# Query stacks of an attention kernel: three heads in four copied straight from the halves, one by DRAM; key steps, the weight step and one subtraction placed anew

## The chip, the core and the metric

One core of a Trainium2 chip runs the whole kernel. TensorE is PE in the profile (PEld is its weight load), VectorE is DVE, ScalarE is ACT, GpSimd is POOL; SyncE, SP, issues nearly all DMAs here, in the order of its program. The metric is the device time of one execution in microseconds (us), the median of several runs.

## The reference, cut to what matters

```
for s in range(4):                       # segments of L = 512 tokens, H = 32 heads of 32
    logits = einsum("bhqd,bhkd->bhqk", qs, ks) * scale + mask      # mask: causal
    a_dot  = softmax(logits) @ vs
    pq     = phi(qs);  a_mem = (pq @ M) / (pq . z + 1e-6)
    o_s    = g * a_mem + (1 - g) * a_dot                            # g = sigmoid(beta), per head
    pk     = phi(ks);  M += pk^T vs;  z += sum(pk)
h  = x + concat(o) @ wo                  # q, k, v = layernorm(x) @ wq, wk, wv
h2 = h + MLP(layernorm(h))               # layernorm, 1024 -> 3584, gelu, 3584 -> 1024
```

All is float32: x has 2048 tokens of 1024 numbers.

## The kernel before, in words

A number is carried as a high part, rounded to the type that PE multiplies fast, and a low part, the rest; a product of two such numbers takes three multiplications (high by high, high by low, low by high). The tokens go in two halves of 1024. Each half has an attention stage and an MLP stage; the change touches only the attention.

An attention stage is a row of 16 units: 8 groups g of four heads, and for each the two segments of the half (sl 0 and 1). `dense` makes the projections of one unit in 24 steps of three 512-column multiplications: steps 0 to 7 keys (kps), 8 to 15 queries (qps), 16 to 23 values (vps). Beside them, step by step, `heads` works the four heads of the unit before: a slot of six steps for each head (`slot`), with the head in three successive slots. The four products of a head's queries and keys (pqk, q0 to q3 in the table, of 128, 384, 256 and 512 columns) stand in its first slot; then come the transposes of the softmax (ptr), and in a third slot the products with the values (av, tile po). PLAN lists what the six steps of a slot hold. For pqk, PE has two banks; DVE frees them (it adds the mask and takes the minimum, mx), ACT then takes the exponential (pr).

The query product needs three multiplications as well. They are done in one by stacking: a query stack has 96 rows, three for each of the 32 numbers of a head, (high, high, low), and the key stack (high, low, high). `stack` builds them. It writes the three sources for all four heads into a DRAM tensor of rows (r, b), three writes of 256 KB, and reads one stack of 96 rows for each head, four reads of 192 KB. The halves (qh, ql, kh, kl) come out of ACT and DVE from qps or kps: `queries` runs at step 16, `keys` at step 8.

The table TIMES says at which of a unit's steps the other work stands (a number of 24 or more lies in the next unit): ks and qs the stacks, kx the turn of phi(k) (DVE transposes in blocks of 32, writes to turn_dram, reads back four times), vx the same for the values (sch<-vps, turn_dram<-sch, sch<-turn_dram), vs the cast of the values' high part on ACT, vl the subtraction for the low part, lk, lq, lv and ck, cq, cv the loads and casts of the next group's weights (wr, wh, and wl on POOL). `weigh`, once in a unit, transposes the softmax denominators rs on PE (pw), writes them to r_dram and reads them back spread over partitions.

The order written in the program isn't the final one. A scheduler places each engine's instructions, DMA issues too, by when it expects their inputs; each engine then runs its own list in order, and waits where an input is late.

Of the kernel before, what the change touches and what calls it, by code (L numbers as in the profile page):

```python
# [17 lines left out]
P = 128  # L18
S = 2048
# [10 lines left out]
RA, RH, RS, PD, PS = 1.3, 14, 0.7, 20, 3  # L30
VT, KT, OT = True, True, True
WLC = 8
TIMES = dict(pk=10, kx=15, pkh=21, pkl=22, ks=16, qs=16, pq=16, pqh=20, pql=20, omt=20, vx=24, pm=25, vs=32, vl=33, pmm=40, om=35, omc=40, od=62, lk=13, lq=16, lv=20, ck=18, cq=22, cv=28)
PLAN = ('r', 'q0', 'a0 S2 t0 q2 s0', 'a1 q1', 't1 w q3', 't2 o s1')
SCALE = DH ** -0.5
EPS = 1e-5
DEN_EPS = 1e-6
# [5 lines left out]
def raw(ap):  # L43
    return ap.bitcast(F32)


def build(tc, x, wq, wk, wv, wo, beta, w1, b1, w2, b2, out):
    nc = tc.nc
# [5 lines left out]
    def ps_dense(name):  # L54
        return psum.tile([P, 512], F32, tag="d", name=name, bufs=3)

    PKL, VSL, GTE, WHK, WHQ, WHV = nc.gpsimd, nc.gpsimd, nc.gpsimd, nc.scalar, nc.vector, nc.scalar
    ident = const.tile([P, P], F32, name="ident")
    make_identity(nc, ident)
    hsel = const.tile([P, 76], F32, name="hsel")[:, 0:4]  # L60
# [23 lines left out]
    o_dram = [dram.tile([NG, P, 512], F32, name=f"o_dram{s}") for s in range(4)]  # L84
# [109 lines left out]
    def hooked(gen, fn, every, count):  # L194
        for n, _ in enumerate(gen):
            if n % every == every - 1 and n // every < count:
                fn(n // every)
            yield
# [152 lines left out]
    def attention(half, first):  # L351
# [4 lines left out]
        def tmp(name):  # L356
            return ab.tile([P, 512], F32, tag="tmp", name=name, bufs=5)
# [3 lines left out]
        def turned(src, to, mid):  # L361

            nc.vector.transpose(mid.rearrange("p (c k d) -> p c k d", c=4, k=4), src.rearrange("p (k c d) -> p c k d", c=4, k=4))
            d = turn_dram[acts.get("turned", 0) % len(turn_dram)]
            acts["turned"] = acts.get("turned", 0) + 1
            nc.sync.dma_start(d, mid)
            for c in range(4):
                nc.sync.dma_start(to[32 * c:32 * c + 32].rearrange("j (h x) -> j h x", h=4),
                                  d[:, c * P:(c + 1) * P].rearrange("(h j) x -> j h x", h=4))

        def tmpr(name):
# [19 lines left out]
        def stack(a, b, name, order):  # L391
            out = []
            n = acts[name] = acts.get(name, 0) + 1
            d = s_dram[name][n % 2]
            for blk, src in enumerate(order):
                nc.sync.dma_start(d[:, blk], raw((a, b)[src]))
            for j in range(4):
                st = ab.tile([96, 512], F32R, tag=name, name=name, bufs=5)
                nc.sync.dma_start(raw(st), d[32 * j:32 * j + 32].rearrange("r b n -> (r b) n"))
                out.append(st)  # L400
            return out

        small = []
# [20 lines left out]
        def dense(g, sl, ws, u):  # L424
# [24 lines left out]
            def key_stack():  # L449
                u["ks"] = stack(v["kh"], v["kl"], "ks", (0, 1, 0))  # L450
# [5 lines left out]
            def key_turn():  # L456
                v["kn"] = scr[1][:, 2 + sl]
                turned(v["pk"], v["kn"], scr[1][:, 0])
# [29 lines left out]
            def query_stack():  # L488
                u["qs"] = stack(v["qh"], v["ql"], "qs", (0, 0, 1))
# [97 lines left out]
            if g < NG - 1:  # L587
                on("od", partial(out_store, u))
                if sl == 1:
                    nxt = u["next"]  # L590
                    for n, w in (("k", wk), ("q", wq), ("v", wv)):
                        on("l" + n, partial(load_weight, nxt, n, w, g + 1))
                        on("c" + n, partial(cast_weight, nxt, n))
# [79 lines left out]
        def weigh(st):  # L673
            u, j = st["u"], st["j"]
            if j < 3:
                return
            n = acts["weighed"] = 1 - acts.get("weighed", 0)
            w = u["w"] = tmp("w") if u["g"] == NG - 1 and u["s"] % 2 else scr[n][:, 1]
            pw = ps_dense("pw")
            nc.tensor.transpose(pw[0:16, 0:P], u["rs"][:, 0:16], ident)  # L680
            nc.scalar.copy(w[0:16, 0:P], pw[0:16, 0:P])
            d = r_dram[n]
            nc.sync.dma_start(d, w[0:16, 0:P])
            for k in range(4):
                nc.sync.dma_start(w[32 * k:32 * k + 32, :],
                                  bass.AP(tensor=d.tensor, offset=d.offset + 512 * k, ap=[[0, DH], [1, 512]]))

        def ptr(st, n):
# [58 lines left out]

        def out_store(u):
            assert u["done"]
            nc.sync.dma_start(o_dram[u["s"]][u["g"]], u["w"])  # L750

        pipe = [None, None]

        def slot(cur):
            p1, p2 = pipe

            def call(st, fn, *args):
                if st:
                    fn(st, *args)

            ops = {"q": (cur, qk), "r": (p1, inverse), "w": (p1, weigh), "t": (p1, ptr), "s": (p1, sub), "S": (p2, sub),
                   "a": (p2, av), "o": (p2, av_out)}
            for step in PLAN:
                for op in step.split():
                    call(ops[op[0]][0], ops[op[0]][1], *[int(c) for c in op[1:]])
                yield
            pipe[0], pipe[1] = cur, p1

        def heads(u):
            for j in range(4):  # L770
                yield from slot({"u": u, "j": j})

        def tail():
            yield from slot(None)
            yield from slot(None)

        def weights(g):
            ws = {}
# [4 lines left out]

        def load_weight(nxt, n, w, g):
            wr = nxt[n] = wp.tile([P, DC, P], F32, tag="wr", name="wr", bufs=2)
            nc.sync.dma_start(wr, w[:, g * P:(g + 1) * P].rearrange("(c p) n -> p c n", p=P))

        def cast_weight(nxt, n):
            wr = nxt[n]
# [8 lines left out]
        for g in range(NG):  # L798
            for sl in range(2):
                u = {"g": g, "s": 2 * half + sl, "T": TIMES, "v": {}, "next": {}}  # L800
                d = dense(g, sl, ws, u)
# [6 lines left out]
                else:  # L808
                    if g == NG - 1 and sl == 1:
                        d = hooked(d, lambda k: load_o(half, 0, k, ab), 3, NG - 1)  # L810
# [647 lines left out]
    for half in range(2):  # L1458
        acts["zt"] = zt = tc.alloc_tile_pool(name=f"zt{half}", bufs=1, side="right")
        attention_pool(half)  # L1460
        first = None if half else opening()
        rest = attention(half, first)
        hts = [lnp.tile([P, D], F32, tag="ln", name="ht0", bufs=4) for _ in range(4)]
        ab = acts["ab"]
# [47 lines left out]
        order = ExitStack()  # L1512
# [84 lines left out]
```

## Time and profile before

| | us |
|---|---|
| median of 3 runs (lowest, highest) | 2323.99 (2323.52, 2328.03) |
| profiled execution | 2326.8 |
| its span, first to last instruction | 2324.9 |
| attention of the first half (about 16 units) | 60 to 549 |
| attention of the second half | 920 to 1400 |
| granted TensorE clock over the span | 0.995 |

In rows of groups, "x128 | 31.2, 244 | 33.7 <-..." reads: 128 instructions, 31.2 us busy, 244 ns each in the mean, 33.7 us in which the engine stood idle just before them, and what ended that idle time. In rows of time the first number is the start in us from the span's start, the second the length; a bracket gives idle time just before. A DMA row on SP (SPq) is the issue alone, "x4" four of them; the transfer itself runs on.

### The profile page before, as it was taken

The numbers are of one execution on the slowest core, as the hardware profiler recorded it, in microseconds if no ns is written. First come the engines' busy times: TensorE is split into PE (matmuls) and PEld (weight loads), VectorE is DVE, ScalarE is ACT, GpSimd is POOL, SyncE is SP. The second block draws the span as 40 slices with busy tenths as digits, with TensorE's granted clock in tenths as the row PEclk, the third lists the DMA queues.
The fourth block names the chain that finished last, engine by engine and source line by source line (L and its number), as shares of the span: only waits on it lengthen the run. The fifth ranks groups of instructions, "written<-read, shape, count | busy, mean of one in ns | idle before, by whom it ended". The sixth has DMA issues, their size and how long they took to land.

```text
span 2324.9 us, 34571 instructions
## 1 busy us (share of the span) xinstructions
PE 2257.8 (97%) x11481; PEld 1863.1 (80%) x11481; DVE 1516.8 (65%) x3041; ACT 1232.6 (53%) x2553; POOL 887.5 (38%) x742
## 2 busy tenths in 40 slices
PE   7999999999999999999999999999999999999999
PEld 6878877777788888788788877788887888888887
DVE  6767777776564565677777776574566666467663
ACT  5767777775363444677777775363344223322221
POOL 4323333333253443333333333244445654155430
PEclk9999999999999999999999999999999999999999
DMA  8656565664475656666666664466567976476772
GB/s 246 193 179 195 182 181 180 186 212 151 151 220 170 198 147 187 207 188 189 186 189 198 199 206 140 163 200 194 154 193 253 350 241 222 145 257 223 246 235 93
DMA packets 406940, 456.26 MB, mean 196 GB/s; under 512 B 30030, under 2 KB 264042, under 8 KB 406762
## 3 DMA queue, kind: packets, MB, share of 16 engines
q1 hardware_dynamic: 343594, 417.34, 57.1%
q10 hardware_dynamic: 63168, 36.71, 5.2%
q8 instruction: 91, 1.49, 0.3%
q14 instruction: 87, 0.71, 0.1%
HBM read 306.28 MB, written 147.65 MB: 195 GB/s over the span
## 4 chain that ended last, share of the span: by engine, by line
PE 73%; DMA 11%; DVE 4%; ACT 4%; POOL 3%; issue 2%; SPq 2%; ACTq 0%; POOLq 0%; DVEq 0%
PE po L1431 19%; PE bps L1035 9%; PE cps L1035 7%; PE dps L1035 6%; PE po L721 4%; PE ppt L701 4%; DMA qs_dram<-ql 3%; PE pqk L651 3%; PE qps L122 2%; PE qps L123 2%; PE qps L124 2%; DMA qs<-qs_dram 2%; PE kps L122 2%; PE kps L123 2%; PE pwo L123 2%
## 5 line engine op out<-in xcount | busy, mean ns | idle before, releaser
L660 ACT ACTIVATE pr<-pr,mx 128x128 f32<-128x128 f32 (+3 forms) x512 | 289.0, 564 | 147.5 <-DVE mx L652 143.2
L652 DVE CUSTOM_DVE_ANT_0 pr<-pqk,mask 128x128 f32<-128x128 f32 (+3 forms) x512 | 246.4, 482 | 107.0 <-PE pqk L651 102.6
L708 DVE TENSOR_TENSOR ptl<-ppt,pth 128x512 fp32r<-128x512 f32 (+1 forms) x384 | 225.7, 596 | 39.0 <-ACT pth L703 35.6
L703 ACT CAST pth<-ppt 128x512 fp32r<-128x512 f32 (+1 forms) x384 | 195.1, 512 | 69.1 <-PE ppt L701 66.0
L701 PE MATMUL ppt<-ident,pr 128*128 128x128 f32 x1280 | 220.7, 278 | 0.0
L651 PE MATMUL pqk<-ks,qs 96*128 96x128 f32 (+3 forms) x512 | 183.5, 360 | 34.5 <-DMA qs<-qs_dram 25.3
L1441 DVE TENSOR_TENSOR c<-c,po 128x512 f32<-128x512 f32 x160 | 105.3, 683 | 149.9 <-PE po L1431 147.3
L701 PEld LDWEIGHTS ppt<-ident,pr 128*128 128x128 f32 x1280 | 165.0, 141 | 35.8 <-issue 1.4
L794 POOL TENSOR_TENSOR wl<-wr,wh 128x1024 fp32r<-128x1024 f32 x42 | 100.3, 2388 | 189.9 <-ACT wh L792 156.4
L721 PE MATMUL po<-ptl,vs 128*64 128x512 f32 (+3 forms) x512 | 154.0, 310 | 0.4 <-DVE ptl L708 0.3
L721 PE MATMUL po<-pth,vs 128*64 128x512 f32 (+3 forms) x512 | 148.1, 310 | 0.7 <-POOL vs L531 0.7
L651 PEld LDWEIGHTS pqk<-ks,qs 96*128 96x128 f32 x512 | 98.5, 193 | 51.7 <-DVE ptl L708 22.8
L1431 PE MATMUL po<-w2h,zh 128*128 128x512 f32 x378 | 120.9, 389 | 0.2 <-DVE zh L1371 0.2
L1288 POOL TENSOR_TENSOR w2r<-w2r 128x512 f32<-128x512 f32 x54 | 87.1, 1625 | 73.8 <-DMA w2r<-in_B_w 73.8
L1035 PE MATMUL bps<-zh,sb 128*128 128x512 f32 x336 | 111.0, 391 | 0.0
L1035 PE MATMUL bps<-zh,sa 128*128 128x512 f32 x336 | 110.8, 390 | 0.0
L122 PE MATMUL kps<-yh,wh 128*128 128x512 f32 (+1 forms) x264 | 109.3, 414 | 0.0
L122 PE MATMUL qps<-yh,wh 128*128 128x512 f32 x256 | 108.0, 422 | 0.1
L122 PE MATMUL vps<-yh,wh 128*128 128x512 f32 x256 | 106.1, 415 | 0.0
L1431 PE MATMUL po<-w2h,hl 128*128 128x512 f32 x322 | 103.1, 390 | 0.2 <-DVE hl L1371 0.2
L123 PE MATMUL kps<-yl,wh 128*128 128x512 f32 (+1 forms) x264 | 102.9, 390 | 0.1
L124 PE MATMUL kps<-yh,wl 128*128 128x512 f32 (+1 forms) x264 | 102.8, 389 | 0.0
(251 smaller groups left out, 6533.6 us busy)
## 6 DMA issues: line engine op xcount, KB each, us to landing
hr<-h_dram SPq DMA_DIRECT2D x112, 448.0 KB, 5.5
w2r<-in_B_w SPq DMA_DIRECT2D x122, 256.0 KB, 4.4
r<-in_B_w SPq DMA_DIRECT2D x56, 512.0 KB, 4.5
ks<-ks_dram SPq DMA_DIRECT2D x128, 192.0 KB, 3.4
qs<-qs_dram SPq DMA_DIRECT2D x128, 192.0 KB, 4.1
h_dram<-ht ACTq DMA_DIRECT2D x84, 256.0 KB, 3.5
ks_dram<-kh SPq DMA_DIRECT2D x64, 256.0 KB, 2.4
qs_dram<-qh SPq DMA_DIRECT2D x64, 256.0 KB, 3.3
```

What stands on the lines that cost most here:

```text
L122: nc.tensor.matmul(ps, ah, bh, start=first, stop=False)
L123: nc.tensor.matmul(ps, ah, bl, start=False, stop=False)
L124: acts["mm"] = nc.tensor.matmul(ps, al, bh, start=False, stop=last)
L651: nc.tensor.matmul(pqk[:, :n], u["qs"][j][:, i * P:(i + 1) * P], u["ks"][j][:, 0:n], start=True, stop=True)
L652: nc.vector.tensor_tensor_reduce(out=st["pr"][:, offs[i]:offs[i] + n], in0=pqk[:, :n], in1=mask[:, 512 - n:512], op0=ALU.add, op1=ALU.min, ...
L660: nc.scalar.activation(pi, pi, AF.Exp, bias=mx[:, i:i + 1], scale=-1.0, accum_out=mx[:, 4 + i:5 + i])
L701: nc.tensor.transpose(ppt[:, o:o + P], pr[:, offs[i] + jk * P:offs[i] + (jk + 1) * P], ident)
L703: acts["pth"] = n, nc.scalar.copy(pth[:, base:base + w], ppt[:, :w])
L708: nc.vector.tensor_tensor(o, x0, x1, op=ALU.subtract)
L721: nc.tensor.matmul(po[:, P * jk:], v, st[part][:, koff[jk]:koff[jk] + w], start=(jk, part) == (0, "pth"), stop=(jk, part) == (2, "ptl"))
L1035: nc.tensor.matmul(ps, x_[:, c, :], y_[:, c, :], start=first and c == 0 and n == 0, stop=last and c == 3 and n == 2, skip_group_check=True)
L1431: nc.tensor.matmul(ps, x_[:, k], y_[k], start=opens and k == 0 and i == 0, stop=closes and k == self.KP - 1 and i == 2, skip_group_check=True)
```

## The change

The query stacks of the first three heads of a unit (QD = 3) are no longer read from DRAM. For each, three DMAs of 32 rows (64 KB) copy a head's rows of qh, qh and ql out of their tiles into every third partition of the stack. For the fourth head, its 32 rows alone are written to the DRAM tensor (three writes of 64 KB) and read back as one stack. That is 13 DMAs a unit in place of 7. Key stacks go by DRAM as before (KD = 0).

The key stack stands at step 11 instead of 16, the key turn at 12 instead of 15. PLAN is replaced by the table HEAD, whose numbers are 6 times the slot, plus the step, plus the place in the step; it holds the same order but for `weigh`, which moves from step 4 to step 3. The values' low part (VSL) is subtracted on DVE instead of POOL. The queue names BQ, TQ, LQ and OQ are all SP, as before.

```
-TIMES = dict(pk=10, kx=15, pkh=21, pkl=22, ks=16, qs=16, ...
-PLAN = ('r', 'q0', 'a0 S2 t0 q2 s0', 'a1 q1', 't1 w q3', 't2 o s1')
+TIMES = dict(pk=10, kx=12, pkh=21, pkl=22, ks=11, qs=16, ...
+HEAD = dict(r=6.1, q0=1.1, a0=14.1, s2=14.2, t0=8.3, q2=2.4, s0=8.5, a1=15.1, q1=3.2, t1=10.1, w=9.2, q3=4.3, t2=11.1, o=17.2, s1=11.3)
+KD, QD = 0, 3
...
-    PKL, VSL, GTE, WHK, WHQ, WHV = nc.gpsimd, nc.gpsimd, nc.gpsimd, nc.scalar, nc.vector, nc.scalar
+    PKL, VSL, GTE, WHK, WHQ, WHV = nc.gpsimd, nc.vector, nc.gpsimd, nc.scalar, nc.vector, nc.scalar
...
-            for blk, src in enumerate(order):
-                nc.sync.dma_start(d[:, blk], raw((a, b)[src]))
+            direct = {"ks": KD, "qs": QD}[name]
             for j in range(4):
                 st = ab.tile([96, 512], F32R, tag=name, name=name, bufs=5)
-                nc.sync.dma_start(raw(st), d[32 * j:32 * j + 32].rearrange("r b n -> (r b) n"))
                 out.append(st)
+                if j < direct:
+                    for blk, src in enumerate(order):
+                        nc.sync.dma_start(raw(st).rearrange("(r b) n -> b r n", b=3)[blk], raw((a, b)[src][32 * j:32 * j + 32, :]))
+            if direct < 4:
+                for blk, src in enumerate(order):
+                    nc.sync.dma_start(d[32 * direct:, blk], raw((a, b)[src])[32 * direct:])
+            for j in range(direct, 4):
+                nc.sync.dma_start(raw(out[j]), d[32 * j:32 * j + 32].rearrange("r b n -> (r b) n"))
...
+            states = [cur] + pipe
+            for step in range(6):
+                for _, op in sorted((t % 6, op) for op, t in HEAD.items() if int(t) % 6 == step):
+                    st = states[int(HEAD[op]) // 6]
+                    if st:
+                        fns[op[0]](st, *[int(c) for c in op[1:]])
```

How the scheduler places it: SP's list, in the second half of a unit of the first attention, from the reads of the key stacks to those of the turned values (sch). Before:

```order
L399 DMA ks<-ks_dram_164 96x512 x3
L368 DMA scl<-turn_dram_157 32x4x128 x4
L399 DMA ks<-ks_dram_164 96x512
L396 DMA qs_dram_166<-qh 128x512 x2
L396 DMA qs_dram_166<-ql 128x512
L399 DMA qs<-qs_dram_166 96x512 x4
L366 DMA turn_dram_158<-sch 128x512
L368 DMA sch<-turn_dram_158 32x4x128 x4
```

And with the change, in the same unit, from the pieces on (the rows ahead are the key reads and scl<-turn_dram):

```order
L403 DMA qs<-qh 32x512 x2
L403 DMA qs<-ql 32x512
L403 DMA qs<-qh 32x512 x2
L403 DMA qs<-ql 32x512
L403 DMA qs<-qh 32x512 x2
L403 DMA qs<-ql 32x512
L406 DMA qs_dram_166<-qh 32x512 x2
L406 DMA qs_dram_166<-ql 32x512
L368 DMA turn_dram_159<-sch 128x512
L691 DMA r_dram_161<-sch 16x128
L408 DMA qs<-qs_dram_166 96x512
L370 DMA sch<-turn_dram_159 32x4x128 x4
```

The three pieces of a head stand together, head by head; the four reads that stood ahead of turn_dram<-sch are one, behind it.

DVE's list, where the low part of the values now stands; pk is phi(k) of the next unit, pr,mx<-pqk the work that frees a bank of pqk. Before, then with the change:

```order
L708 TENSOR_TENSOR ptl<-ppt,pth 128x512
L388 SCALAR_TENSOR_TENSOR pk,zc<-e,r 128x512
L652 ISA pr,mx<-pqk,mask 128x256
L652 ISA mx 128x1
L363 STREAM_TRANSPOSE scl<-pk 128x512
```

```order
L716 TENSOR_TENSOR ptl<-ppt,pth 128x512
L390 SCALAR_TENSOR_TENSOR pk,zc<-e,r 128x512
L539 TENSOR_TENSOR vs<-sch,vs 128x16x32
L660 ISA pr,mx<-pqk,mask 128x256
L660 ISA mx 128x1
```

The subtraction vs<-sch,vs stands behind pk and ahead of a pqk.

ACT's list in the same place: vs<-sch is the cast that the subtraction needs. Before, then with the change:

```order
L444 CAST kh<-kps 128x512
L527 CAST vs<-sch 128x16x32
L703 CAST pth<-ppt 128x512
L382 ACTIVATE e<-kps 128x512
L383 ACTIVATE r<-kps 128x512
L660 ACTIVATE pr,mx<-pr,mx 128x384
```

```order
L452 CAST kh<-kps 128x512
L711 CAST pth<-ppt 128x512
L384 ACTIVATE e<-kps 128x512
L385 ACTIVATE r<-kps 128x512
L535 CAST vs<-sch 128x16x32
L668 ACTIVATE pr,mx<-pr,mx 128x384
```

The cast moved back behind three instructions.

More of the change, by code (lines that the diff above doesn't have):

```diff
@@ L32 @@
 WLC = 8
-TIMES = dict(pk=10, kx=15, pkh=21, pkl=22, ks=16, qs=16, pq=16, pqh=20, pql=20, omt=20, vx=24, pm=25, vs=32, vl=33, pmm=40, om=35, omc=40, od=62, lk=13, lq=16, lv=20, ck=18, cq=22, cv=28)
-PLAN = ('r', 'q0', 'a0 S2 t0 q2 s0', 'a1 q1', 't1 w q3', 't2 o s1')
+TIMES = dict(pk=10, kx=12, pkh=21, pkl=22, ks=11, qs=16, pq=16, pqh=20, pql=20, omt=20, vx=24, pm=25, vs=32, vl=33, pmm=40, om=35, omc=40, od=62, lk=13, lq=16, lv=20, ck=18, cq=22, cv=28)
+HEAD = dict(r=6.1, q0=1.1, a0=14.1, s2=14.2, t0=8.3, q2=2.4, s0=8.5, a1=15.1, q1=3.2, t1=10.1, w=9.2, q3=4.3, t2=11.1, o=17.2, s1=11.3)
+KD, QD = 0, 3
 SCALE = DH ** -0.5
@@ L55, in ps_dense @@
         return psum.tile([P, 512], F32, tag="d", name=name, bufs=3)
-    PKL, VSL, GTE, WHK, WHQ, WHV = nc.gpsimd, nc.gpsimd, nc.gpsimd, nc.scalar, nc.vector, nc.scalar
+    PKL, VSL, GTE, WHK, WHQ, WHV = nc.gpsimd, nc.vector, nc.gpsimd, nc.scalar, nc.vector, nc.scalar
+    BQ, TQ, LQ, OQ = nc.sync, nc.sync, nc.sync, nc.sync
     ident = const.tile([P, P], F32, name="ident")
@@ L365, in turned @@
             acts["turned"] = acts.get("turned", 0) + 1
-            nc.sync.dma_start(d, mid)
+            TQ.dma_start(d, mid)
             for c in range(4):
-                nc.sync.dma_start(to[32 * c:32 * c + 32].rearrange("j (h x) -> j h x", h=4),
+                TQ.dma_start(to[32 * c:32 * c + 32].rearrange("j (h x) -> j h x", h=4),
                                   d[:, c * P:(c + 1) * P].rearrange("(h j) x -> j h x", h=4))
@@ L682, in weigh @@
             d = r_dram[n]
-            nc.sync.dma_start(d, w[0:16, 0:P])
+            BQ.dma_start(d, w[0:16, 0:P])
             for k in range(4):
-                nc.sync.dma_start(w[32 * k:32 * k + 32, :],
+                BQ.dma_start(w[32 * k:32 * k + 32, :],
                                   bass.AP(tensor=d.tensor, offset=d.offset + 512 * k, ap=[[0, DH], [1, 512]]))
@@ L749, in out_store @@
             assert u["done"]
-            nc.sync.dma_start(o_dram[u["s"]][u["g"]], u["w"])
-        pipe = [None, None]
+            OQ.dma_start(o_dram[u["s"]][u["g"]], u["w"])
+        stages = int(max(HEAD.values())) // 6
+        pipe = [None] * stages
+        fns = {"q": qk, "r": inverse, "w": weigh, "t": ptr, "s": sub, "a": av, "o": av_out}
         def slot(cur):
[L755 to L765, printed above, removed]
+            states = [cur] + pipe
[4 more added lines that the diff above has]
+                        fns[op[0]](st, *[int(c) for c in op[1:]])
                 yield
-            pipe[0], pipe[1] = cur, p1
+            pipe[:] = states[:-1]
         def heads(u):
@@ L773, in tail @@
         def tail():
-            yield from slot(None)
-            yield from slot(None)
+            for _ in range(stages):
+                yield from slot(None)
         def weights(g):
@@ L785, in load_weight @@
             wr = nxt[n] = wp.tile([P, DC, P], F32, tag="wr", name="wr", bufs=2)
-            nc.sync.dma_start(wr, w[:, g * P:(g + 1) * P].rearrange("(c p) n -> p c n", p=P))
+            LQ.dma_start(wr, w[:, g * P:(g + 1) * P].rearrange("(c p) n -> p c n", p=P))
         def cast_weight(nxt, n):
```

## The prediction

> **What bounds the kernel now.** I read the page's busy times first, then the busy times by stage, then the groups of instructions kept apart by shape.
>
> ```profile
> span 2324.9 us, 34571 instructions
> PE 2257.8 (97%) x11481; PEld 1863.1 (80%) x11481; DVE 1516.8 (65%) x3041; ACT 1232.6 (53%) x2553; POOL 887.5 (38%) x742
> 60.00:549.00 489.00, 464.85 (x2736) 384.34 (x2735) 352.24 (x981) 351.88 (x882) 157.16 (x163) 0.99 0.61 186
> 920.00:1400.00 480.00, 466.79 (x2755) 387.62 (x2755) 350.61 (x1009) 353.28 (x880) 167.10 (x164) 1.00 0.65 197
> L651 PE MATMUL pqk<-ks,qs 96*128 96x128 f32 x128 | 31.2, 244 | 33.7 <-DMA qs<-qs_dram 25.3 <-DVE ptl L708 7.2 <-PE qps L123 0.8
> ```
>
> TensorE (PE) sets the time: 97% busy over the span. The two long rows are the attention of the two halves; their first five numbers after the length are the busy times of PE, PEld, DVE, ACT and POOL. In both stages DVE and ACT are near 73%, and PE is idle for 489.00 - 464.85 = 24.2 and 480.00 - 466.79 = 13.2 us. The last row says where nearly all of it is: before the 128-column pqk product, which opens a head (128 heads, 128 rows), PE stood 33.7 us. The reader should see that the first head of a unit waits for its query stack. The next rows show one such case: DVE and PE first, then the DMA queue of SP (time, length, what).
>
> ```profile
> 249.21 0.47 PE L651 MATMUL pqk<-ks,qs 96*128 96x512 f32 x1
> 248.89 0.68 DVE L484 TENSOR_TENSOR ql<-qps,qh 128x512 fp32r<-128x512 f32 x1
> 259.47 0.40 PE L124 MATMUL kps<-yh,wl 128*128 128x512 f32 x1
> 261.60 0.30 PE L651 MATMUL pqk<-ks,qs 96*128 96x128 f32 x1 [1.73 <-DMA qs<-qs_dram]
> 248.05 1.87 SPq L368 DMA_DIRECT2D scl<-turn_dram  x4
> 250.02 2.92 SPq L399 DMA_DIRECT2D ks<-ks_dram  x4
> 253.03 0.85 SPq L396 DMA_DIRECT2D qs_dram<-qh  x2
> 253.98 0.45 SPq L396 DMA_DIRECT2D qs_dram<-ql  x1
> 254.52 0.91 SPq L786 DMA_DIRECT2D wr<-in_A_wk  x1
> 258.88 1.73 SPq L399 DMA_DIRECT2D qs<-qs_dram  x4
> 260.65 0.43 SPq L366 DMA_DIRECT2D turn_dram<-sch  x1
> ```
>
> The query halves are complete at 248.89 + 0.68 = 249.6. SP issues the key reads first, writes the halves to DRAM at 253.0 to 254.4, stands until they have landed, and reads the first stack at 258.9; PE, ready at 259.87, starts at 261.60. So the budget from ql to PE's arrival is 259.87 - 249.57 = 10.3 us, and the route takes 12.0. The 7.2 us that the group row puts to DVE ptl I count to the same DMA: nothing in the pqk product reads ptl.
>
> **The change part by part.** First the DMA prices (KB each, median us from issue to landing), since SBUF to SBUF doesn't occur in this trace.
>
> ```profile
> qs<-qs_dram SPq DMA_DIRECT2D x128, 192.0 KB, 4.1
> qs_dram<-qh SPq DMA_DIRECT2D x64, 256.0 KB, 3.3
> sch<-turn_dram SPq DMA_DIRECT2D x128, 64.0 KB, 2.4
> scl<-r_dram SPq DMA_DIRECT2D x64, 64.0 KB, 2.1
> wr<-in_A_wv SPq DMA_DIRECT2D x16, 512.0 KB, 5.2
> ```
>
> Direct pieces. A piece is 64 KB of 2 KB rows into 32 partitions. Its nearest row is scl<-r_dram, the same size and rows: 2.1 us; the upper end is the larger read, 4.1. One issue costs 1.73 / 4 = 0.43 us of SP. Between ql and the last of the first head's three pieces the new order has up to four other issues: three of scl and the fourth key read, which waits until PE is done with the third head before (its last pqk at 249.21, about when ql is). So that piece is issued by 4 x 0.43 + 0.43 = 2.2 us after ql and lands at 4.3 to 6.3. Against a budget of 10.3 that is 4 to 6 us early, and the whole wait of 33.7 goes, apart from the 0.8 put to qps. I take 25.3 + 7.2 = 32.5 us off. The second and third heads need theirs six and twelve steps later, the fourth eighteen; a stage of 489 us holds 16 units of 24 steps (1.3 us a step), so the fourth has 10.3 + 18 x 1.3 = 34 us, and its DRAM route of about 5.2 us of issues, 3.3 of writing and 4.1 of reading ends long before.
>
> SP's load. Per unit 13 issues replace 7: 6 x 0.43 = 2.6 us more. Cover: SP stood from 255.4 (254.52 + 0.91) to 258.88, 3.5 us, for the landing of qs_dram, which no longer holds it. The value turn (turn_dram<-sch) was issued at 260.65, behind the four query reads; now one read, or none, is ahead. What waits anew on SP is that one read, for the landing of the three 64 KB writes; behind it stand the value's reads, which wait for turn_dram<-sch anyhow. I take nothing, with bounds of 1 us a unit either way only if that cover is gone. Moving the key stack to step 11 and the key turn to 12 lifts the key reads (2.92 us here, right ahead of the query writes) out of the way; that is what lets the pieces start at once, and is counted in the 2.2.
>
> Lower half of V on DVE. The rows around it:
>
> ```profile
> L531 POOL TENSOR_TENSOR vs<-sch,vs 128x512 fp32r<-128x512 f32 x32 | 41.6, 1300 | 97.1 <-ACT vs L527 97.1
> L527 ACT CAST vs<-sch 128x512 fp32r<-128x512 f32 x32 | 19.8, 620 | 19.8 <-DMA sch<-turn_dram 19.7
> L388 DVE SCALAR_TENSOR_TENSOR pk<-e,r x24: 691/693/1771, 29.4 to 1342.7; 128x512 f32<-128x512 f32 x24
> 300.93 2.40 POOL L794 TENSOR_TENSOR wl<-wr,wh 128x1024 fp32r<-128x1024 f32 x1 [8.53 <-ACT wh L792]
> 303.28 1.29 POOL L531 TENSOR_TENSOR vs<-sch,vs 128x512 fp32r<-128x512 f32 x1
> 303.74 1.38 DVE L388 SCALAR_TENSOR_TENSOR pk<-e,r 128x512 f32<-128x512 f32 x1 [0.23 <-ACT r L383]
> 268.39 0.62 ACT L527 CAST vs<-sch 128x512 fp32r<-128x512 f32 x1 [1.10 <-DMA sch<-turn_dram]
> 269.09 1.29 POOL L531 TENSOR_TENSOR vs<-sch,vs 128x512 fp32r<-128x512 f32 x1 [7.33 <-ACT vs L527]
> 277.65 0.40 PE L721 MATMUL po<-pth,vs 128*64 128x512 f32 x1
> ```
>
> POOL loses 41.6 us; DVE gains 32 subtractions. The nearest DVE instruction with both inputs in SBUF is pk: 0.69 alone, 1.38 where it met POOL's vs. I take 0.69, 22 us in all; the upper end, 1.38, is 44. Both lie on an engine with (489.00 - 352.24) + (480.00 - 350.61) = 266 us free in the two stages. PE's first use of vs comes 277.65 - 270.38 = 7.3 us after POOL's end here, so the result isn't late. What is new is that the mask-and-minimum instructions for pqk stand behind vs on DVE, and vs behind ACT's cast, which waited 19.7 us in total for the value's way through DRAM. I charge 0.1 us a unit, 3 us, as an estimate between nothing and rival two's full price.
>
> [...]
>
> The weight's transpose pw, one step earlier, needs rs:
>
> ```profile
> 261.54 0.22 POOL L670 TENSOR_TENSOR rs<-rs,gate 128x16 f32<-128x16 f32 x1
> 267.10 0.27 PE L680 MATMUL pw<-ident,rs 128*16 128x128 f32 x1
> ```
>
> PE's pw comes 5.3 us after rs is ready (261.76); one step (1.3) and the removed wait (1.7) leave 2.3. Its five DMAs go with it, on a queue with 3.5 us to spare. Nothing; if the cover went, a stall of under 1 us in each of 32 units.
>
> Sum: 2324.9 - 32.5 + 3.0 = 2295.4 span. The profiled execution is 2326.8, 1.9 more than its span, hence 2297.3; it stands 2.8 above the median of 2323.99, so on the median's scale 2294.5.
>
> **The rivals.** One: half the gain is lost at the weights. In some units SP issues wr<-in_A_wv only behind nine pieces and three writes: 2.2 + 9 x 0.43 = 6.1 us after ql, landing 5.2 later, at 11.3. ACT casts it close to the unit's end (10.3). If the cast's stall of about 1 us passed to PE in every unit that loads weights or starts after it (16 of 32), 16 us return: 2310. For it: ACT is in order and the exponentials are behind it. Against: the new order has moved that cast later too.
>
> Two, slower: the value's subtraction holds DVE. PE gains 33.7 / 32 = 1.05 us a unit, the value's DRAM way doesn't, so ACT's wait grows from 19.7 / 32 = 0.62 to at most 1.67; DVE is then held with it, plus 0.69, and PE's two pqk banks aren't freed. If all 1.67 + 0.69 = 2.4 pass to PE, it loses 32 x 2.4 = 76 and gains 32.5: 2367; if half, 2329. It turns slower where more than 1.0 us a unit passes. For it: DVE had not this wait before. Against:
>
> ```profile
> 264.23 0.44 PE L651 MATMUL pqk<-ks,qs 96*128 96x384 f32 x1
> 265.77 0.28 PE L651 MATMUL pqk<-ks,qs 96*128 96x256 f32 x1
> 267.13 0.48 PE L651 MATMUL pqk<-ks,qs 96*128 96x512 f32 x1
> L651 PE MATMUL pqk<-ks,qs 96*128 96x512 f32 x128 | 61.8, 483 | 0.8 <-DVE mx L652 0.8
> ```
>
> PE's pqk come about 1.4 us apart and two may be outstanding, so DVE may be some 2.9 us late, and DVE's mx cost PE 0.8 us in all so far.
>
> Three, the change doesn't do what it says: a piece from SBUF to SBUF lands only after about 10 us, against 2.1 to 4.1. Then the first head waits as now (2.2 + 9.8 = 12.0) and the time stays at 2324.
>
> Four: the pieces run one after another. Nine pieces and three writes at 2.1 hold the DMA engines for 25 us after ql; the value's turn behind them, issued 11.1 after ql now, comes 14 us late, 7 more than the 7.3 that PE has: 32 x 7 = 224, about 2515. Against it: the four 64 KB reads of a group are issued within 1.87 us, and the median of such reads, from its own issue, is 2.1 to 2.4; one after another the fourth would need 8, so they overlap. [...]
>
> **How the numbers follow.** Forecast 0.62, 2294.5. Rival one 0.17, two 0.12, three 0.06, four 0.03. About 0.2% (4.6 us) is what a measurement of this kernel can tell from no change. Forecast and rival one are faster: 0.79; rival three is the same: 0.06; two and four slower: 0.15. The range: at the low end all 33.7 go and nothing returns, 2324 - 34 = 2290, with 6 more out of the 8.3 us of the next two rows (waits of PE: us, times, longest), which lie around the ends of the attention stages, where the change moves the heads among the output products: 2284.
>
> ```profile
> PE pwo L123 <- POOL zl L99: 4.9, 3, 2.5
> PE pwo L122 <- ACT zh L98: 3.4, 2, 2.1
> ```
>
> The high end takes in rival one and part of a weak form of two, 2320, and leaves out rivals three, four and the rest of two, 0.2.
>
> **What would show it.** Right: the idle time before the 96x128 pqk falls from 33.7 to under 3, the two attention stages shorten by about 29 together and nothing else does; pieces land within 2 to 4 us. Wrong: pqk still waits for a DMA (rival three); new idle time of PE before pqk or ppt put to DVE mx or ACT pth, with ACT's wait for sch<-turn_dram above 50 us (two); SP's pieces landing over 6 us after issue (four); ACT's cast wh waiting for wr<-in_A_wv (one).

## The result and the profile after

The changed kernel takes 2272.17 us in the median of 4 runs (2270.84 to 2274.44); the kernel before, on the same chip, 2326.01 (2323.52 to 2331.02). The ratio is 0.9767, with a 95% interval of 0.9747 to 0.9787: 53.8 us less. The forecast was 29.5 us less; the time lies below the range's low end of 2284. The profiled execution after is the one of 2274.44.

First the page's busy times and the group row that carried the prediction.

```profile
span 2272.7 us, 34849 instructions
PE 2243.7 (99%) x11481; PEld 1861.9 (82%) x11481; DVE 1541.0 (68%) x3073; ACT 1232.8 (54%) x2553; POOL 856.8 (38%) x710
L659 PE MATMUL pqk<-ks,qs 96*128 96x128 f32 x128 | 28.9, 226 | 1.1 <-DVE mx L660 1.1
```

The idle time before the first product of a head fell from 33.7 to 1.1 us, and no DMA is named there any more. But the span fell by 52.2, not by 32.6. PE's idle time as a whole went from 2324.9 - 2257.8 = 67.1 to 2272.7 - 2243.7 = 29.0, so by 38.1; and its busy time fell by 14.1 although the number of matmuls is the same, 11481. That second part is what the prediction had no term for.

The waits of PE after (us, times, longest) show what is left of the idle time:

```profile
PE pt L277 <- ACT xt L267: 9.7, 2, 8.5
PE pwo L124 <- ACT wh L100: 3.4, 2, 2.2
PE pwo L125 <- POOL zl L101: 2.5, 2, 1.3
PE po L729 <- DVE ptl L716: 1.9, 2, 1.1
PE pwo L125 <- POOL wl L101: 1.6, 2, 1.3
PE po L729 <- DVE ot L740: 1.6, 3, 0.9
PE po L729 <- DVE vs L539: 1.2, 2, 0.8
```

The output products (pwo) wait 3.4 + 2.5 + 1.6 = 7.5 us. Before they waited 13.9: 4.9 and 3.4 in the two rows of the prediction, and 3.0, 1.5 and 1.1 in these three:

```profile
PE pwo L122 <- ACT wh L98: 3.0, 2, 1.5
...
PE pwo L123 <- DVE wl L99: 1.5, 2, 0.8
PE pwo L123 <- POOL wl L99: 1.1, 1, 1.1
```

Most of the busy time that went is in the granted clock. In the traces of the kernels before and after it changes only on a grid of 3.41 us (the last section has the evidence). These are such stretches in the profile of before; after the length come the busy times of PE, PEld, DVE, ACT and POOL, then the clock.

```profile
161.11:164.52 3.41, 1.37 (x6) 0.76 (x5) 2.42 (x7) 1.71 (x5) 0.21 (x1) 1.00 0.20 65
164.52:167.94 3.42, 2.49 (x7) 1.72 (x8) 0.30 (x2) 0.49 (x2) 0.00 (x0) 0.50 0.83 238
1116.85:1120.26 3.41, 1.75 (x13) 1.70 (x14) 1.33 (x6) 1.02 (x3) 0.00 (x0) 1.00 0.82 208
1120.26:1123.67 3.41, 3.41 (x26) 3.00 (x25) 2.97 (x10) 2.63 (x8) 0.00 (x0) 1.00 0.35 117
```

In the first stretch PE was busy for 1.37 of 3.41 us, since it waited for a query stack, and in the next the clock is 0.50. In the third it was busy for 1.75, a little more than half, and the clock stays at 1.00 in the fourth. The trace's record of the clock has 23.9 us at half speed before, in six places (seven windows of 3.4 us), and 6.8 after, in two. I count 3.4 us of matmuls at half speed for 1.7, an estimate from the clock of 0.50. So (23.9 - 6.8) / 2 = 8.5 us of the busy time went with the stops behind which it stood. Four of the seven windows, 6.8 us of the 8.5, stood behind waits for a query stack: two behind the first row here, one behind each of the others.

```profile
165.45 0.45 PE L651 MATMUL pqk<-ks,qs 96*128 96x128 f32 x1 [2.96 <-DMA qs<-qs_dram]
515.36 0.30 PE L651 MATMUL pqk<-ks,qs 96*128 96x128 f32 x1 [3.29 <-DMA qs<-qs_dram]
938.62 0.52 PE L651 MATMUL pqk<-ks,qs 96*128 96x128 f32 x2 [2.54 <-DMA qs<-qs_dram]
```

The other three stood behind output products. Of the two that are left after, one stands behind an output product, and this one behind a product with the values (po) and an output product together:

```profile
509.40:512.80 3.40, 1.61 (x12) 0.98 (x10) 2.49 (x8) 3.35 (x8) 2.12 (x1) 1.00 0.03 7
512.80:516.20 3.40, 3.11 (x7) 2.48 (x8) 1.32 (x1) 0.12 (x2) 0.24 (x1) 0.50 0.55 149
```

The other timed runs bear it out. In the 54 executions of the kernel before that were timed beside the experiments the granted clock is 0.991 to 0.997, in the nine of the changed kernel 0.997 to 1.0. One less the clock, times the span, is about 13 us in the mean of the first and 4 of the second.

Where along the run the time went can be read off the first MLP product, which follows the last output product of each half. Before:

```profile
634.37 0.39 PE L1035 MATMUL cps<-zh,wh 128*128 128x512 f32 x1
...
1512.93 0.39 PE L1035 MATMUL cps<-zh,wh 128*128 128x512 f32 x1
```

After:

```profile
606.03 0.39 PE L1040 MATMUL cps<-zh,wh 128*128 128x512 f32 x1
...
1463.27 0.39 PE L1040 MATMUL cps<-zh,wh 128*128 128x512 f32 x1
```

The first half reaches its MLP 28.3 us earlier, the second 49.7, so 21.4 came in the second attention (the second half's first kps starts 28.3 us earlier, as the first MLP did); of the 52.2 only 2.5 came in the last MLP.

Last, of the kernel after, the transfers (KB each, median us from issue to landing); the issue of a piece and the value's subtraction by line (ns, least, median, most); and the groups of the value's cast and subtraction:

```profile
qs<-qh SPq DMA_DIRECT2D x192, 64.0 KB, 2.0
...
turn_dram<-sch SPq DMA_DIRECT2D x32, 256.0 KB, 2.3
...
qs<-qs_dram SPq DMA_DIRECT2D x32, 192.0 KB, 3.9
```

```profile
L403 SPq DMA_DIRECT2D qs<-qh x192: 506/588/1727, 34.3 to 1345.8; - x192
```

```profile
L539 DVE TENSOR_TENSOR vs<-sch,vs x32: 678/688/1371, 58.0 to 1366.0; 128x512 fp32r<-128x512 f32 x32
```

```profile
L535 ACT CAST vs<-sch 128x512 fp32r<-128x512 f32 x32 | 19.8, 618 | 3.8 <-DMA sch<-turn_dram 3.7
L539 DVE TENSOR_TENSOR vs<-sch,vs 128x512 fp32r<-128x512 f32 x32 | 22.7, 708 | 1.0 <-issue 0.4 <-ACT vs L535 0.2
```

A piece lands in 2.0 us, just under the lower bound of 2.1; its issue takes 0.59 us of SP, not 0.43. ACT's wait for the value did not grow from 19.7, as rival two had it, but fell to 3.7.

### The profile page after: what moved, and what is told of

Its sections match the earlier page's. It is cut to its first block, busy times and chain, and to the rows that moved or that the text cites. A ratio compares the mean times of both kernels' runs of the same rounds, so it can differ in the third digit from the quotient of the medians.

```text
span 2272.7 us, 34849 instructions
## 1 busy us (share of the span) xinstructions
PE 2243.7 (99%) x11481; PEld 1861.9 (82%) x11481; DVE 1541.0 (68%) x3073; ACT 1232.8 (54%) x2553; POOL 856.8 (38%) x710
## 4 chain that ended last, share of the span: by engine, by line
PE 86%; DMA 4%; POOL 3%; ACT 2%; DVE 2%; issue 1%; SPq 1%; POOLq 0%; ACTq 0%; DVEq 0%
PE po L1436 22%; PE bps L1040 10%; PE cps L1040 7%; PE dps L1040 7%; PE po L729 6%; PE ppt L709 5%; PE pqk L659 3%; PE qps L124 3%; PE qps L125 2%; PE kps L124 2%; PE qps L126 2%; PE vps L124 2%; PE kps L126 2%; PE kps L125 2%; PE vps L125 2%; PE vps L126 2%
```

## The experiments

The runs are compared by their ratio to the kernel before, timed on the same chip. For each profiled execution the table has the span, PE's idle time (span less PE's busy time), the time at half clock, and PE's busy time less half of that: the work at full clock. The end of a run, where PE is done, is left out. Taking half off is an approximation; the short and long stops below show how far it goes.

| kernel | ratio (95%) | span | PE idle | at half clock | work at full clock |
|---|---|---|---|---|---|
| before | 1 | 2324.9 | 67.1 | 23.9 | 2245.9 |
| changed | 0.9767 (0.9747 to 0.9787) | 2272.7 | 29.0 | 6.8 | 2240.3 |
| changed, again | 0.9763 (0.9746 to 0.9780) | 2273.4 | 30.9 | 3.4 | 2240.8 |
| pieces alone | 0.9785 (0.9762 to 0.9809) | 2282.7 | 33.9 | 17.1 | 2240.3 |
| all but pieces | 0.9895 (0.9870 to 0.9920) | 2303.8 | 52.7 | 10.2 | 2246.0 |
| key steps alone | 0.9937 (0.9915 to 0.9960) | 2312.3 | 58.2 | 17.1 | 2245.5 |
| all but key steps | 0.9763 (0.9749 to 0.9777) | 2273.0 | 28.6 | 6.8 | 2240.9 |
| all but V on DVE | 0.9766 (0.9751 to 0.9782) | 2277.6 | 33.1 | 6.8 | 2241.1 |
| throwaway matmuls in before | 1.0007 (0.9989 to 1.0024) | 2328.2 | 65.5 | 20.5 | 2252.4 |
| short stops | 1.0016 (1.0001 to 1.0032) | 2330.4 | 58.2 | 13.7 | 2265.4 |
| long stops | 1.0075 (1.0054 to 1.0096) | 2349.1 | 77.1 | 51.2 | 2246.4 |
| four heads by pieces | 0.9895 (0.9877 to 0.9913) | 2304.5 | 51.1 | 20.5 | 2243.1 |
| the same, weights held | 1.0049 (1.0031 to 1.0068) | 2341.4 | 70.9 | 54.6 | 2243.2 |
| the same, V on POOL | 0.9892 (0.9872 to 0.9912) | 2296.6 | 45.2 | 17.1 | 2242.8 |

**Pieces alone.** The changed kernel with the key steps, the weight step and V's subtraction put back:

```
-TIMES = dict(pk=10, kx=12, ..., ks=11, ...
+TIMES = dict(pk=10, kx=15, ..., ks=16, ...
-HEAD = dict(..., w=9.2, ...)
+HEAD = dict(..., w=10.2, ...)
-    PKL, VSL, ... = nc.gpsimd, nc.vector, ...
+    PKL, VSL, ... = nc.gpsimd, nc.gpsimd, ...
```

> Before with the direct pieces alone (QD = 3); keys at 16 and 15, the weight step at 4 and the subtraction on POOL as before. Theory A (the pieces are the gain; what comes beyond the removed wait is clock): idle before the 96x128 pqk from 33.7 to under 6, time 35 to 53 us less than before. Rival B (the key reads ahead of the query writes on SP were the cause, so moving them is the gain): the pieces still stand behind 2.9 us of key reads, the wait halves at best, 10 to 25 us less.

Measured: 0.9785, about 50 us less than before. The row of the first head:

```profile
L659 PE MATMUL pqk<-ks,qs 96*128 96x128 f32 x128 | 28.9, 226 | 0.3 <-DVE mx L660 0.2 <-DMA qs<-ql 0.2
```

The pieces alone take the whole wait away; the three other edits add at most a few us on top (0.9767 and 0.9763 against 0.9785, with intervals that overlap).

**All but the pieces** (QD = 0 in the changed kernel), and **the key steps alone** (QD = 0 again, with the weight step and V's subtraction put back as well: only kx=12 and ks=11 are kept).

> The changed kernel with all four stacks by DRAM again (QD = 0); keys, weight step and subtraction stay moved. Theory A: the route of 12.0 us from ql loses at most the 2.9 us of the key reads ahead, so some wait stays: 12 to 15 us idle before pqk, time 15 to 30 us less than before. Rival B: nearly the whole gain, 40 us or more, idle before pqk under 5.

> Before with ks at 11 and kx at 12 alone. Theory A: within 5 us of all_but_direct, since the weight step and the subtraction on DVE carry nothing. Rival C (the subtraction on DVE carries part: it frees POOL and shortens the value's way): 8 us or more slower than all_but_direct.

Measured: 0.9895 and 0.9937, some 25 and 15 us less than before. Their first-head rows, in this order:

```profile
L659 PE MATMUL pqk<-ks,qs 96*128 96x128 f32 x128 | 30.2, 236 | 14.0 <-DMA qs<-qs_dram 8.0 <-DVE sch L365 2.9 <-DVE rs L675 1.7
```

```profile
L659 PE MATMUL pqk<-ks,qs 96*128 96x128 f32 x128 | 30.8, 240 | 22.6 <-DMA qs<-qs_dram 9.1 <-DVE ptl L716 3.9 <-DVE mx L660 3.6
```

With the key reads out of the way the old DRAM route loses a third of the wait, with all three edits more than half. The gains do not add: 50 for the pieces and 25 for the three others give 55 together, since both take the same wait away. The two runs here differ by 10 us, where theory A had at most 5 and rival C at least 8; the difference is known to about 8 us, so it decides between them no further than that the weight step and V's subtraction may carry something while the DRAM route stands.

**All but the key steps; all but V on DVE.** Beside them the changed kernel was run again, on the same chip.

> The changed kernel once more, as the measure for the three beside it. Both theories expect a ratio to the kernel before of 0.9767 within its interval (0.9747 to 0.9787). Theory A (the time is PE's idle time plus half of the time at half clock) expects the trace to close: its full-clock matmul time within 3 us of the first trace's, whatever the stops. If the pieces alone (ratio 0.9785) are all that counts, this run and they differ by under 0.3%.

> The changed kernel with only the key steps put back where they were (key turn 15, key stack 16). Theory A, a budget: the pieces already arrive before PE asks for them, as in the run of the pieces alone (0.2 us of waiting), so the key steps' own gain (15 us when done alone) has nothing left to remove: ratio within 0.003 of the changed kernel, idle before q0 under 1.5. Theory B, the parts add: 15 us slower than the changed kernel, ratio 0.983 to 0.984.

> The changed kernel with only the lower half of V put back on GpSimd. Theory A: with the first heads' stalls gone PE comes to the output products sooner, and V's slower route shows there: po waits for POOL vs about 3.6 us as in the run of the pieces alone, so 2 to 5 us slower than the changed kernel (ratio +0.001 to +0.002). Theory B (the subtraction on DVE, in front of the masks of pqk, costs about as much as it saves; the prediction charged 3 us for it): equal or up to 3 us faster than the changed kernel. Theory C (V on DVE carries the 10 us by which the three other edits together beat the key steps alone): 8 to 10 us slower.

Measured: 0.9763, 0.9763 and 0.9766. Neither edit can be told from nothing once the pieces are there. The differences between these runs are known to about 5 us, so an effect of 2 to 5 us from V's engine is neither shown nor ruled out; one of 8 to 10 is out. The wait itself came as expected: po waits 3.8 us for POOL's vs, against 0.9 for DVE's.

**Throwaway matmuls in the kernel before.** Ten matmuls into the product's own bank, ahead of the product, in the three units in which a half clock had stood behind a wait for the query stack:

```
+FILL, NFILL = ((0, 2, 0), (0, 7, 1), (1, 0, 0)), 10
...
+            if (i, j) == (0, 0) and (half, u["g"], u["s"] % 2) in FILL:
+                for _ in range(NFILL):
+                    nc.tensor.matmul(pqk, u["ks"][0][:, 0:P], u["ks"][0], start=True, stop=True)
```

> Before with ten throwaway 512-column products of the key stack into the pqk bank ahead of the first head's pqk, in the three units where PE stood longest (3.0, 3.3 and 2.5 us); nothing else is changed and no wait is shortened. Theory A (a long idle stretch of PE is followed by 3.4 us or twice that at half clock): the half clock at 164.5 (6.8 us), 516.1 (3.4) and 939.4 (3.4) goes, 13.6 us at half speed, so the time falls by 5 to 7 us although the stacks come no earlier. Rival D (the half clock comes by itself, whatever PE does): it stays, time within 2 us of before.

Measured: no time gained, 1.0007. Taken by the time alone, that is what rival D forecast, and theory A's 5 to 7 us did not come. In the profiled execution the half clock after the stop at 162 us was gone, and from that unit to the next the run gained another 3.4 us on before. But half clocks stood behind other stops, at 443, 521, 535, 600 and 1409 us, 20.5 us in all, and the 30 matmuls cost 2252.4 - 2245.9 = 6.5 us of PE's time. The granted clock of the 12 executions, 0.993 to 0.996, is no higher than before. So filling three stops by place did not take the half clocks away: the run speaks for the clock's cost at one place and settled nothing more. Hence the next two.

**Short stops and long stops.** In the last MLP stage of the changed kernel, which has hardly a stop of its own, one throwaway matmul and two copies before each of 48 products (STEP, COPIES = 1, 2), or one and twelve before each of 16 (3, 12):

```
+            if opens and 12 < self.np <= 60 and self.np % STEP == 0:
+                nc.tensor.matmul(ps, ah[:, 0], bh[0], start=True, stop=True)
+                for _ in range(COPIES):
+                    nc.scalar.copy(junk, ps[:, 0:64])
```

> The changed kernel with 48 short stops of PE put into the last stage of the MLP, one before each of 48 output products: one throwaway matmul into the product's bank (0.39 us, as the 128x512 matmuls there) and two small ScalarE copies of that bank that the product must wait for. The result is not touched. Estimate from the 16x128 copy's 255 ns: about 0.8 to 1.1 us of idle each, 38 to 53 in all, and 19 us of throwaway matmuls. Clock theory (a stop draws a half-clock stretch of 3.4 us only where PE is idle for over 1.7 us of one 3.41 us window of a fixed grid): no or hardly any half-clock stretch in the stage, and the added span equals added idle plus 19 us. Rival (each stop costs its idle and something for starting again, whatever its length): added span over idle plus 19 us by 48 times the same amount, 0.5 us or more a stop if it is to explain the missing 14 us of the first comparison.

> As the short stops, but 16 stops, each of one throwaway matmul and twelve copies: estimate 2.7 to 3.4 us of idle each, 43 to 55 in all, and 6 us of throwaway matmuls. Clock theory: a stop of 3 us has over 1.7 us within one window of the grid in about nine cases of ten, so 12 to 16 half-clock stretches of 3.4 us, each costing 1.7: 20 to 27 us on top of idle plus 6. Rival (no such rule, the half clock only goes along with other things): no more half-clock stretches than the changed kernel has (0 in this stage), and added span equal to idle plus 6 us.

Against the changed kernel run again (span 2273.4), the long stops add 75.7 us to the span: 46.2 of idle, 23.9 for 47.8 us more at half clock, 5.6 of work. The stretches came behind 12 of the 16 stops, two of them twice as long; 20 to 27 us were expected for them. The short stops add 57.0: 27.3 of idle (0.57 each, shorter than estimated), 5.1 at half clock, and 24.6 of work. Of their three windows more, two stand behind one longer stop in the stage, 2.9 us from 2118 us on, and one at 495 us, outside of it. So the clock theory's count, 12 to 16, was met where long stops were put in.

Of what the 24.6 us are made, one of the short stops shows; the second of these rows is the throwaway matmul.

```profile
1926.41 0.39 PE L1442 MATMUL po<-zh,zh 128*128 128x512 f32 x1
1926.64 0.39 PE L1436 MATMUL po<-w2h,zl 128*128 128x512 f32 x1
1927.63 0.50 PE L1442 MATMUL po<-w2h,zl 128*128 128x512 f32 x1 [0.60 <-ACT hsel L1438]
1927.96 0.40 PE L1442 MATMUL po<-w2l,zl 128*128 128x512 f32 x1
```

The matmul in the flow gave way to the next after 0.23 us (1926.41 to 1926.64). The one with nothing behind it shows its whole 0.39, so 0.16 more, and the first behind the stop gave way only after 0.33 (1927.63 to 1927.96), 0.10 more. So this stop cost 0.26 us beyond its idle time: with the 0.23 of the throwaway matmul that is 0.49, 48 times 0.49 is 23.5, and 24.6 was measured. The 5.6 us of the long stops seem to be less, 0.35 each. But there half of the half clock is too much to take off. At half clock such a matmul gave way after 0.43 us, not 0.46,

```profile
2084.57 1.06 PE L1442 MATMUL po<-zh,hl 128*128 128x512 f32 x2
2085.43 0.63 PE L1442 MATMUL po<-zl,hl 128*128 128x512 f32 x1
```

which is 47% lost, and PE was busy for 49.2 of the 51.2 us. With 47% of PE's busy time at half clock taken off in both kernels, the long stops cost 8.0 us of work, 0.50 each, and agree with the short ones.

**Four heads by pieces.** QD = 4 in the changed kernel, so that nothing of the queries goes through DRAM.

> The changed kernel with all four heads of a stack sent as 64 KB pieces, none by DRAM rows. Theory A (SP's queue has room: it stands several us a unit): within 0.1% of the changed kernel, since the fourth head was not late; pieces still land in 2.0 us. Theory B (the issues of pieces at 0.59 us are what fills SP now): three more pieces a unit in place of three writes and a read hold the value turn back by 3 x 0.59 - 4 x 0.42 = 0.1 us, nothing, but without the wait for the DRAM rows SP runs ahead, so up to 3 us faster. Theory C (pieces crowd the DMA engines): 12 pieces a unit land later than 2.5 us and q0 waits again, 5 us or more slower.

Measured: 0.9895, about 31 us slower than the changed kernel; none of the three theories. Pieces still land in 2.0 us, so they do not crowd. PE's new waits:

```profile
PE pqk L659 <- DVE mx L660: 9.5, 7, 1.9
PE ppt L709 <- DVE ptl L716: 6.8, 11, 0.9
PE po L729 <- DVE ptl L716: 3.3, 3, 1.4
```

ACT waits 31.2 us for sch<-turn_dram, the value's read. The SP queue shows where about half of that comes from. This is one of four units alike in this kernel's second half, then the same place in the changed one, run again, and under the first's SP rows those of POOL and ACT:

```profile
1058.82 0.57 SPq L368 DMA_DIRECT2D turn_dram<-sch  x1
1064.73 0.37 SPq L791 DMA_DIRECT2D wr<-in_A_wq  x1
1065.19 1.95 SPq L370 DMA_DIRECT2D sch<-turn_dram  x4
1062.30 2.41 POOL L799 TENSOR_TENSOR wl<-wr,wh 128x1024 fp32r<-128x1024 f32 x1 [3.15 <-ACT wh L797]
1070.73 0.62 ACT L535 CAST vs<-sch 128x512 fp32r<-128x512 f32 x1 [3.74 <-DMA sch<-turn_dram]
```

```profile
1047.00 0.34 SPq L368 DMA_DIRECT2D turn_dram<-sch  x1
...
1050.01 1.75 SPq L370 DMA_DIRECT2D sch<-turn_dram  x4
1052.35 0.40 SPq L791 DMA_DIRECT2D wr<-in_A_wq  x1
```

A read of the next query weights has moved ahead of the value's four reads. It needs the weight buffer that POOL's wl frees at 1062.30 + 2.41 = 1064.71, and goes out at 1064.73; the value's reads, ready for some 4 us if their write landed in the median 2.4, stand behind it, and ACT, in order, stands at the cast. In these four units ACT stands 3.3 to 3.8 us each; the rest of the 31.2 lies in other units and is not explained by this. Two runs tested it.

The first adds a dependence by which that weight read (wq) stands behind the last of the value's reads:

```
-                turned(ps["v"], v["vn"], scr[0][:, 0])
+                read = turned(ps["v"], v["vn"], scr[0][:, 0])
+                if "wq" in acts:
+                    tc.add_manual_dep(acts.pop("wq").ins, read.ins.name, NOSYNC, reason="program order")
...
+            if n == "q":
+                acts["wq"] = op
```

> Four heads sent as pieces (which alone made it 31 us slower than the changed kernel), and the read of the next query weights, wr<-in_A_wq, held behind the value's four reads on SP's queue. Theory A (the loss is one of order: without the fourth head's DRAM read in the way, that weight read moved ahead of the value's reads in 11 units and waits there for a free weight buffer; the value's reads then start 8 us after its write to DRAM instead of 4.4): ACT's wait for sch<-turn_dram falls from 31.2 to under 12 us and the ratio to 0.976 to 0.980. Theory B (the pieces themselves, 12 in a unit at 0.59 us, are too many): the ratio stays at 0.988 to 0.990.

The second puts V's lower half back on POOL, with the four heads by pieces:

> Four heads sent as pieces, the weight read left ahead of the value's reads, but the lower half of V back on GpSimd. Theory A with rival two of the prediction (the late value holds the subtraction on DVE, and the masks of pqk and ptl behind it): PE's new waits for DVE mx and ptl (19.6 us together) fall under 6, ACT's wait for sch<-turn_dram stays near 30, PE waits for vs instead by under 8; ratio 0.979 to 0.985. If ACT's wait alone is what hurts (the cast of vs stands ahead of the exponentials): ratio stays 0.987 to 0.991.

Holding the weights: ACT's wait for the value fell from 31.2 to 7.0 us and PE's waits for mx and ptl from 19.6 to 3.7, as the theory of order has it. But the ratio is 1.0049, slower than before the change: the dependence held the weights back far longer than meant, and PE now stands before the query products.

```profile
PE qps L126 <- POOL wl L804: 21.7, 14, 1.7
PE qps L124 <- DVE wh L802: 16.2, 13, 2.4
```

So PE's new waits go when the value comes in time, but PE stood elsewhere meanwhile, which gives the value time too; that the order alone carries the 31 us is not shown, and both ratios expected for this run were missed. V on POOL: 0.9892, no recovery; ACT still waits 26.2, and PE for mx and ptl 14.7. So the subtraction on DVE is not what holds the rest; that ACT's cast is, remains an argument. No version beat the changed kernel.

## Why the prediction was right and wrong

**The bound and the budget: right.** PE did wait for the first head's stack, and the pieces come in time. With the pieces alone the wait falls from 33.7 to 0.3. Charging the 7.2 us under "DVE ptl" to the DMA was right too: in that run they are gone with it.

**The sum: the step that failed** is "I take 25.3 + 7.2 = 32.5 us off". The idle time it names did go, 32.6 of it, but the stops here cost more than their idle time, and the sum had no term for that. Term by term, forecast and measured span:

| term | forecast | measured |
|---|---|---|
| idle before the first head | -32.5 | -32.6 |
| new waits in attention (charge) | +3.0 | +4.4 |
| idle of the output products | 0 (6 in the low end) | -6.4 |
| other idle time | 0 | -3.5 |
| time at half clock | 0 | -8.5 |
| work at full clock | 0 | -5.6 |
| sum | -29.5 | -52.2 |

The charge stands against waits of po and ppt: 1.1 us before and 5.5 after (1.9, 1.6 and 1.2 in the rows above, the rest in shorter ones). Only 1.2 of it names the subtraction that the charge was for, so that the sizes agree is in part luck.

The half clock is the largest term left out, and the page had it: a granted clock of 0.995 over 2324.9 us is 11.6 us, and the prediction never asked which stops that came from. The work at full clock is about 5 us lower in each kernel in which three heads go by pieces (2240.3 to 2241.1, against 2245.5 to 2246.0 with none). PE had 53 stops of over 0.05 us before and 27 after; at the 0.26 us of the short stops' rows, 26 stops are 6.8 us. With the half clock counted as for the long stops, the two last terms are -7.5 and -6.6, so the price of a stop accounts for the work term, though by rows of another stage.

The output products' 6.4 us stood in the low end only, as a thing that the new head order might bring. With the pieces alone they still wait 11.6 us (6.1, 4.0 and 1.5), with the key steps alone 13.9, as before. They wait 8.5 without the pieces, 6.8 without the key steps and 6.9 without V on DVE. So none of these three edits is needed for it, and what these last three runs have in common is the weight step, pw one step earlier. That points to the weight step, which the prediction priced at nothing; it was not run alone, so how it does it stays open.

**The range** took 6 of these 8.3 us and all of the 33.7 as its best case, so its low end of 2284 counted idle time only. With the clock's 11.6 us in it, it would have reached 2272.4, about the time measured.

**The single prices.** Pieces: 2.0 us, forecast 2.1 to 4.1. Their issue was mis-sized, 0.59 against 0.43, without consequence at nine a unit. V on DVE: 22.7 us, forecast 22; its longest is 1.37 us. That one ran beside an instruction of POOL (1.29 us from 1365.56) and ended 0.54 us after it; so did the prediction's pk of 1.38 us, 0.55 after POOL's vs (303.28 + 1.29). In the trace after the change no subtraction began while a wl ran, so what the 2.40 us of a wl beside it would cost was not shown. The earlier key steps, of which the prediction says "that is what lets the pieces start at once", did not matter for the pieces: put back, they cost nothing that could be measured.

**The rivals.** One: ACT's casts do wait for wr<-in_A_wv,

```profile
L797 ACT CAST wh<-wr 128x1024 fp32r<-128x1024 f32 x28 | 29.4, 1048 | 10.7 <-DMA wr<-in_A_wv 8.9 <-PE kps L125 1.7
```

8.9 us in all, but PE's list of waits has none for it. Two did not come: the value's write landed in 2.3 us, against 4.1 before,

```profile
turn_dram<-sch SPq DMA_DIRECT2D x32, 256.0 KB, 4.1
```

and ACT's wait for it fell. A loss of the rival's kind lies close by, though: one more head by pieces brought a wait of 31.2 us there and lost 31 us, and moving the subtraction off DVE, where the rival had it, gave nothing back. Three and four are out by the 2.0 us: a piece is issued in 0.59 and lands in the median 2.0, so the nine overlap; one after another they would need 18.

## What to carry to other kernels

Price a stop of the bounding engine, here PE, by three things: its idle time, some 0.26 us for running out and starting again (one short stop's rows), and, where a half clock follows, 1.6 to 1.7 us for each 3.41 us of it; in these traces one followed every window of the grid with 1.95 us or more of PE's idle time, and 15 of 35 with 1.6 to 1.95. Read the granted clock and look for its dips at the stops that you mean to remove: here the half clocks behind the waits for the query stack went with those waits. And a wait on SP's list, which SP works in order, also held what stood behind it: with the fourth head's read taken away the weight read moved up, and the value's reads went out 6.4 us after the issue of their write (1058.82 to 1065.19) in place of 3.0 (1047.00 to 1050.01). So look at which transfer then stands ahead of the next thing that an engine needs.

## What the runs showed of the hardware

In the traces of the kernels before and after, every stretch of the granted clock, at full or at half speed, lasts a whole number of times 3.413 us (1 or 2 at half speed, 4 to 515 at full), but for the last, which the end of the run cuts. In each of the 14 traces all half-speed stretches start on one grid of such windows, to less than 0.05 us, and the grid's place against the start of the span differs from trace to trace. Laid on that grid, the matmul records of the 14 traces have 79 half-speed windows (left out are the ends of the runs and their first 20 us, where PE has hardly begun and the trace's record of the clock starts only at 13 to 19 us). Every window with 1.95 us or more of idle, 50 of them, was followed by one; of those with 1.6 to 1.95 us, 15 were and 20 were not; of the 14 half-speed windows behind less idle than that, 11 follow another half-speed window. I had not expected so short a stop to do it: the six stretches of the kernel before stand behind stops of 1.5 to 3.3 us, the two shortest with another of 0.8 us close behind. PE had work in each of the windows ahead of these six, 0.74 us in the one with the least and 1.70 in the one with the most.

A 64 KB piece from SBUF to SBUF took 2.0 us to land, close to a read of 64 KB from DRAM (2.3 for scl<-turn_dram in the same trace), but 0.59 us to issue, where a read took 0.43.
